# Lightning attention in front of an MLP: attention two chunks at a time on 64x64 PE tiles, 512-byte loads of k and v in one gated sequence, and dummy matmuls from the moment the identity exists

## The chip, the cores and the metric

One core of one Trainium2 chip. The metric is device time in microseconds of one execution (lower is better). All runs told here ended in the state "fast", but for one of the six with 256-byte runs, which is left out of its figures; the granted TensorE clock is 0.985 to 1.0 in the profiles, and the two places below 0.998 are named. A kernel's time is the median of its runs. Faster or slower needs more than 2%. The engines are PE (TensorE, matmuls), DVE (VectorE), ACT (ScalarE), POOL (GpSimd) and SP (SyncE, which issues transfers).

## The reference, cut to what matters

Causal linear attention with a decay per head, then a two-layer MLP over its output. Batch 4, 8 heads, 768 positions, head width 64; the MLP goes 512 → 2048 → 512 over 3072 tokens. All inputs and the output are float32.

```python
# attention, block by block of 64 positions (lam is one decay per head)
intra = einsum('bhic,bhjc->bhij', qb, kb) * Dmask        # lam^(i-j) for i >= j, else 0
intra = einsum('bhij,bhjd->bhid', intra, vb)
inter = einsum('bhid,bhde->bhie', qb * lam_pow, kv_state)
out   = intra + inter
kv_state = lam_block * kv_state + einsum('bhsd,bhse->bhde', kb * rev_pow, vb)
...
# MLP
h = x @ w_in
g = where(h >= 1, h, where(h <= -1, 0, (h + 1)**2 / 4))
out = g @ w_out
```

## The kernel before

Attention works on 24 chunks of 128 positions (six to a batch entry), the MLP on six stages of 512 tokens (four chunks). q is multiplied by lam^pos and k by lam^-pos while they are cast to bf16 (`cast_q`, `cast`), so that a plain causal mask suffices and the state is a plain sum. k and q are then transposed: by matmuls with an identity for the first six chunks, by DMA later. `xT` is the attention output, transposed, as the MLP reads it.

The kernel fixes the order itself: each operation is entered in a list with its engine, an estimated duration, what it needs and a due time, and a small list scheduler in Python fixes the order on each engine. Each engine's program then has its instructions in this order. What the change touches:

```python
ORDER = [0, 1, 2, 3, (0, 0), (0, 1), (0, 2), (0, 3), 4, (1, 0), ...]   # loads: chunks, (0,i) = w_in parts, (1,i) = w_out parts
PARTS = {1: 4, 2: 2, 3: 2, 4: 1}                 # MLP stage -> into how many token parts layer 1 is cut
L0 = [(0, 0), (0, 1), (1, 0), (1, 1), (0, 2), (1, 2), (0, 3), (1, 3)]   # stage 0: (half of the tokens, quarter of w_in)
...
def f_s2(c):                                     # scores of one chunk: two row tiles of 64 x 128
    for hp in range(HP):
        for hi in range(2):
            nc.tensor.matmul(pst[c, hi][:, hp, :], lhsT=kT[c][HD[hi], hp, :], rhs=q_cols(c, hp, HD[hi]), ...)

def f_o(c):                                      # output of one chunk: 4 + 8 full-array matmuls, block-diagonal operands
    for hp in range(HP):
        if cb > 0:
            nc.tensor.matmul(po[:, hp], lhsT=ubd[(c - 1) % NUB][:, hp, :], rhs=q_cols(c, hp), ...)
        for hi in range(2):
            nc.tensor.matmul(po[:, hp], lhsT=vi[c % NV][:, hp, hi].rearrange("p a d -> p (a d)"), rhs=sc_sb[c][:, hi, hp, :], ...)

def f_u(c):                                      # state: 4 matmuls, summed in PSUM over the whole batch entry
    for hp in range(HP):
        nc.tensor.matmul(pu[0][:, hp, :], lhsT=pair(ks[c], hp), rhs=v_pair(vi[c % NV], hp), ...)

def f_x(c):                                      # ACT: the output of chunk c goes to its columns of the stage's xT
    if sx not in xT:
        xT[sx] = xp.tile([128, KO, MS], BF16, name="xT", tag="xT")
    nc.scalar.copy(out=xT[sx][:, :, off:off + C]..., in_=pot[c]...)

def f_l1(s, ni, n, tok):                         # MLP layer 1
    for j in range(n):
        for ko in range(KO):
            nc.tensor.matmul(ph[:, j * m:(j + 1) * m], lhsT=w_in_sb[:, ko, ...], rhs=xT[s][:, ko, tok], ...)

def f_load(c, x, wait):                          # k and v after the first pair: per chunk, 64 floats = 256 bytes a run
    d = nc.sync.dma_start(out=t, in_=(k, v)[x - 1][b, :, s0:s0 + C, :].rearrange("h p d -> p h d"))
```

Of the kernel before, what the change touches and what calls it, by code (L numbers as in the profile page):

```python
# [23 lines left out]
def kernel(  # L24
# [18 lines left out]
    C = 128  # L43
# [12 lines left out]
    LD = 6  # L56
# [3 lines left out]
    DX, DLEAD = 16, 6000  # L60
# [3 lines left out]
    XT, NQT, NQK, RING = 6, 4, 4, 3  # L64
    W_IN = (4, 4, 4, 4)
    W_OF = [i for i, n in enumerate(W_IN) for _ in range(n)]
    ORDER = [0, 1, 2, 3, (0, 0), (0, 1), (0, 2), (0, 3), 4, (1, 0), (1, 1), 5, (1, 2), (1, 3)]
    PF = (0,)
    D0 = (8350, 11900, 15450, 19000)
    FIRST = [(0, 2), (2, 4)]  # L70
    L0 = [(0, 0), (0, 1), (1, 0), (1, 1), (0, 2), (1, 2), (0, 3), (1, 3)]
    GATE = {(0, 0): ("lq", 1), 4: 1, 6: 5}
    LORD = {0: (0, 1, 2), 2: (0, 1, 2)}
# [10 lines left out]
    scp = ctx.enter_context(tc.tile_pool(name="scp", bufs=3))  # L84
    xp = ctx.enter_context(tc.tile_pool(name="xp", bufs=3))
    xsp = ctx.enter_context(tc.tile_pool(name="xsp", bufs=2))
# [7 lines left out]
    pp_u = ctx.enter_context(tc.tile_pool(name="pp_u", bufs=1, space=PS))  # L94
    pp_s = ctx.enter_context(tc.tile_pool(name="pp_s", bufs=1, space=PS))
    pp_o = ctx.enter_context(tc.tile_pool(name="pp_o", bufs=1, space=PS))

# [12 lines left out]
    pos_i = const.tile([128, 2, NCB], I32)  # L110
    nc.gpsimd.iota(pos_i[:, 0], pattern=[[C, NCB]], base=-S // 2, channel_multiplier=1)
    nc.gpsimd.iota(pos_i[:, 1], pattern=[[1, 2], [2 * C, NCB // 2]], base=-S // 2, channel_multiplier=2)
# [4 lines left out]
    for e in range(2):  # L117
# [4 lines left out]
    causal = const.tile([128, 128], F32)  # L122
    nc.gpsimd.memset(causal, 1.0)
    nc.gpsimd.affine_select(
        out=causal, in_=causal, compare_op=AX.is_ge, fill=0.0,
        base=0, pattern=[[1, 2], [2, 64]], channel_multiplier=-1)


    NKB, NUB, NV = 2, 3, 4
    kbd = [const.tile([128, HP, 2, 128], BF16, name=f"kbd{i}") for i in range(NKB)]  # L130
    ubd = [const.tile([128, HP, 128], BF16, name=f"ubd{i}") for i in range(NUB)]
    vi = [const.tile([128, HP, 2, 2, D], BF16, name=f"vi{i}") for i in range(NV)]
# [4 lines left out]
    for t in vi[:2]:  # L137
        nc.vector.memset(t, 0.0)
    rest = const.tile([1, 3, H], F32)
    nc.scalar.activation(out=rest[:, 0], in_=lam_r, func=AF.Ln)  # L140
    pos = const.tile([128, 2, NCB], F32)
# [7 lines left out]
    ln_lam = ln_ps[:, 0, :H]  # L149
    for i in range(3):  # L150
        nc.tensor.matmul(ln_lam, lhsT=ones, rhs=piece[:, i], start=(i == 0), stop=(i == 2))
    nc.scalar.copy(vi[2], vi[0])
    arg = const.tile([128, 2, NCB, H], F32)
    nc.vector.tensor_tensor(arg.rearrange("p a c h -> p (a c) h"), _bc(pos.rearrange("p a c -> p (a c)"), 2, H),
                            _bc(ln_lam, 1, 2 * NCB), op=AX.mult)
    for t in ubd[:2]:
        nc.vector.memset(t, 0.0)
    tab_q = const.tile([128, 2, NCB // 2, H], F32)
    nc.scalar.activation(out=tab_q.rearrange("p a c h -> p (a c) h"), in_=arg[:, 1], func=AF.Exp)
    tab_p = const.tile([128, 2, 2, H], F32)  # L160
    nc.scalar.activation(out=tab_p.rearrange("p e m h -> p e (m h)"),
                         in_=arg[:, 1].rearrange("p (e m) h -> p e (m h)", e=2)[:, :, :2 * H], func=AF.Exp, scale=-1.0)
    tab_k = const.tile([128, NCB, H], F32)
    nc.scalar.activation(out=tab_k, in_=arg[:, 0], func=AF.Exp, scale=-1.0)
    nc.scalar.copy(vi[3], vi[1])
    tab_qn = const.tile([128, NCB, H], F32)
    causal_n = const.tile([128, 128], F32)

    def late_setup():
        nc.scalar.activation(out=tab_qn, in_=arg[:, 0], func=AF.Exp)  # L170
        nc.gpsimd.memset(causal_n, 1.0)
        nc.gpsimd.affine_select(out=causal_n, in_=causal_n, compare_op=AX.is_ge, fill=0.0,
                                base=0, pattern=[[1, 128]], channel_multiplier=-1)

    def v_out(t):

        a = list(t[:, 0, 0, 0, :].ap)
        return bass.AP(t.tensor, t[:, 0, 0, 0, :].offset, [a[0], [4 * D, HP], [3 * D, 2], [1, D]])

    def v_pair(t, hp):  # L180

        x = t[:, hp, 0, 0, :]
        return bass.AP(t.tensor, x.offset, [list(x.ap)[0], [3 * D, 2], [1, D]])

    def v_rows(t, hp, rows):

        x = t[rows, hp, 0, 0, :]
        return bass.AP(t.tensor, x.offset, [list(x.ap)[0], [3 * D, 2], [1, D]])
# [33 lines left out]
    MMS, FETCH = {"s": 8, "o": 12}, 1300  # L222
    FIRST_BYTE = 2350
    LDD, QXD, KXD, STD = 20000, 7000, 7000, 3000
    ON_POOL, ON_DVE = (1,), ((0, 1),)
    W_AFTER = {1: ("cq", 1, 1)}

    def run_plan(free):
# [25 lines left out]
        while len(out_seq) < len(ops):  # L254
# [12 lines left out]
            if x.dma:  # L267
                dma_free = max(dma_free, t + (1300 if e == "SP" else 2100)) + x.dma
                x.end = dma_free + (400 if x.key[0] in ("ld", "lq") and x.key[1] < (CPS if x.key[0] == "ld" else CPS // 2) else 1000 if x.key[:2] == ("w", 0) else 1400)
                if x.key[0] in ("ld", "lq") and x.key[1] >= (FAR if x.key[0] == "ld" else FAR // 2):  # L270
                    x.end += SLACK if (x.key[1] if x.key[0] == "ld" else 2 * x.key[1]) >= 10 else NEAR
                if e == "SP":
                    xfer.append(dma_free)
            out_seq.append((t, len(out_seq), x))
            for u in users[x.key]:
                left[u.key] -= 1
                if left[u.key] == 0:
                    ready[u.eng].append((max(y.t if y.eng == u.eng and y.key != u.gate else y.end + (XSL if u.eng == "SP" and y.eng == "POOL" and u.dma in (640, 1280) else LAT) for y in u.needs), u))
        for t, _, x in sorted(out_seq, key=lambda p: p[:2]):
            if DBG:  # L280
                print(f"{t / 1e3:9.3f} {x.due / 1e3:9.3f} {x.eng:5s} {x.ns:6.0f} {x.key}")
            x.fn()

    def mm(*cols):
        return sum(c / 2.4 + 3 for c in cols)
# [3 lines left out]
    pu = [None]  # L289
# [5 lines left out]
    def cast(c, eng):  # L295
        ks[c] = qkp.tile([128, H, D], BF16, name="ks", tag="ks")
        tab = tab_p[:, c % 2, c // 2] if c // 2 in PF else tab_k[:, c % NCB, :]
        eng.tensor_tensor(ks[c], qkv_ld[c, 1], _bc(tab, 2, D), op=AX.mult)  # L298

    def cast_q(m, e, eng):  # L300
        if e == 0:
            qs[m] = qsp.tile([128, 2, H, D], BF16, name="qs", tag="qs")
        qs[m, e] = qs[m][:, e]
        if 2 * m >= DX:
            eng.tensor_tensor(qs[m, e], qkv_ld[m, 0][:, e], _bc(tab_qn[:, (2 * m + e) % NCB, :], 2, D), op=AX.mult)  # L305
            return
        eng.tensor_tensor(qs[m, e], qkv_ld[m, 0][:, :, e], _bc(tab_q[:, e, m % (NCB // 2), :], 2, D), op=AX.mult)  # L307
# [6 lines left out]
    def q_cols(c, hp, rows=slice(0, 128)):  # L314

        i = c % 2
        if c >= DX:
            return qT[c // 2][rows, i, hp, :]
# [3 lines left out]
    vn, x_sb = {}, {}  # L322

    def cast_v(c):
        if c == CPS:
            late_setup()
        if c >= DX:
# [38 lines left out]
    def last_of(a):  # L366

        return a | 1 if a // 2 in PF else a

# [435 lines left out]
```

## Time and profile before

| | before |
|---|---|
| median of 3 runs | 219.13 us (218.85 to 219.54) |
| span in the profile | 217.3 us |
| first MLP matmul starts | 18.9 us |
| last matmul ends | 214.1 us |
| PE busy | 204.9 us, 94% |

The main views are shown and read in the prediction. Two more are needed for the comparison. First, the work by stretches of the kernel before, from the first MLP matmul on. The columns of the work by stretches are the stretch, its length, then the busy time (and the number of instructions) of PE, PE weight loads, DVE, ACT and POOL, the granted clock, the DMA share and GB/s; those of the order of time are start, duration, instruction, count, and in brackets the idle time before it with what ended it.

```profile
18.90:36.60 17.70, 16.87 (x170) 14.15 (x171) 13.71 (x21) 13.62 (x26) 8.20 (x10) 1.00 1.22 216
36.60:214.20 177.60, 177.24 (x1505) 110.13 (x1504) 113.43 (x174) 100.40 (x176) 43.04 (x37) 1.00 0.77 153
```

From 36.6 us on PE is idle for only 0.36 us in 177.6. What it loses, it loses before.

### The profile page before, as it was taken

Reading aid. Unit: us, or ns where it says so; the run is one execution under the profiler, and the core shown is the slowest. Engines: PE = TensorE matmul, PEld = TensorE weight load, DVE = VectorE, ACT = ScalarE, POOL = GpSimd, SP = SyncE. Lnnn points to the kernel's source line nnn. Section 1 sums busy time; section 2 is a strip of 40 time slices with the busy share of each in tenths; the row PEclk is TensorE's granted clock in tenths of the full one; section 3 lists DMA queues with packets and bytes.
Section 4 is the critical chain, followed back from the end, with each engine's and each line's share of the span. In section 5 each row is a group of like instructions: output and inputs, shape, how many; then the busy total and the mean of one; then the engine's idle time right before and its main releaser. Section 6 shows DMA issues by size and latency. Waiting matters only on the chain.

```text
span 217.3 us, 4494 instructions
## 1 busy us (share of the span) xinstructions
PE 204.9 (94%) x1803; PEld 132.8 (61%) x1803; DVE 139.4 (64%) x221; ACT 124.5 (57%) x222; POOL 62.3 (29%) x69
## 2 busy tenths in 40 slices
PE   0589899999999999999999999999999999999994
PEld 0378787778558777777767776744545544444442
DVE  5685697869926796958858776632688655554301
ACT  7457678357637677577657657635864544555030
POOL 5590096037533464341409200343000000000000
DMA  6999999989998999999998346999784301110122
GB/s 166 277 214 207 252 172 217 214 178 214 179 227 153 250 154 238 158 241 220 196 249 199 67 83 137 218 191 221 231 138 169 88 12 48 48 48 7 45 97 97
DMA packets 95974, 35.42 MB, mean 163 GB/s; under 512 B 78418, under 2 KB 93010, under 8 KB 95954
## 3 DMA queue, kind: packets, MB, share of 16 engines
q1 hardware_dynamic: 91728, 30.94, 69.9%
q0 software_dynamic: 4224, 4.19, 12.0%
q8 instruction: 14, 0.23, 0.5%
q14 instruction: 6, 0.05, 0.1%
q10 hardware_dynamic: 2, 0.00, 0.0%
HBM read 27.26 MB, written 6.29 MB: 154 GB/s over the span
## 4 chain that ended last, share of the span: by engine, by line
PE 92%; DMA 2%; ACT 2%; DVE 1%; issue 1%; POOL 1%; DVEq 0%; POOLq 0%
PE ph L481 39%; PE py L529 36%; PE po L439 3%; PE ps L409 3%; PE pu L380 2%; DMA x0f<-in_q_dram 2%; PE po L436 1%; PE py L523 1%; PE pt L336 1%; PE po L431 1%; PE po L457 1%; PE py L343 1%; PE po L428 1%; POOL qs L307 1%; ACT r L490 1%
## 5 line engine op out<-in xcount | busy, mean ns | idle before, releaser
L481 PE MATMUL ph<-xT,w_in_sb 128*128 128x256 bf16 (+2 forms) x768 | 95.7, 273 | 0.9 <-ACT xT L469 0.7
L490 ACT ACTIVATE r<-ph,one 128x512 bf16<-128x512 f32 x96 | 65.9, 688 | 46.3 <-PE ph L481 28.9
L529 PE MATMUL py<-w_out_sb,gT 128*128 128x512 bf16 x368 | 89.9, 379 | 0.0
L481 PEld LDWEIGHTS <-w_in_sb 128*128 128x128 bf16 x768 | 63.2, 98 | 23.9 <-issue 1.3
L529 PEld LDWEIGHTS <-gT 128*128 128x128 bf16 x368 | 34.9, 98 | 34.5
L500 DVE TENSOR_SCALAR t<-r 128x1024 bf16<-128x1024 bf16 x48 | 24.2, 505 | 35.8 <-ACT r L490 35.7
L506 DVE TENSOR_TENSOR w<-r,t 128x1024 bf16<-128x1024 bf16 x48 | 38.6, 803 | 1.4
L511 DVE TENSOR_TENSOR gT<-w,t 128x1024 bf16<-128x1024 bf16 x48 | 37.4, 780 | 1.7
L298 POOL TENSOR_TENSOR ks<-x1f,tab_k 128x512 bf16<-128x512 f32 x20 | 25.0, 1256 | 26.1 <-DMA x1f<-in_k_dram 20.5
L534 ACT COPY osb<-py 128x512 f32<-128x512 f32 x23 | 13.5, 586 | 17.7 <-PE py L529 16.4
L307 POOL TENSOR_TENSOR qs<-x0f,tab_q 128x512 bf16<-128x512 f32 x15 | 17.1, 1156 | 21.1 <-DMA x0f<-in_q_dram 15.9
L384 ACT CAST ubd<-pu 64x256 bf16<-64x256 f32 x40 | 14.6, 366 | 8.1 <-PE pu L380 5.2
L305 POOL TENSOR_TENSOR qs<-x0f,tab_qn 128x512 bf16<-128x512 f32 x8 | 9.0, 1126 | 28.6 <-DMA x0f<-in_q_dram 21.2
L421 DVE TENSOR_TENSOR sc<-ps,causal 128x512 bf16<-128x512 f32 x12 | 8.3, 689 | 9.5 <-PE pt L409 9.4
L469 ACT CAST xT<-po 128x512 bf16<-128x512 f32 x15 | 8.8, 584 | 8.8 <-PE po L439 5.2
L439 PE MATMUL po<-sc,vi 128*128 128x128 bf16 x112 | 10.5, 219 | 0.0
L439 PEld LDWEIGHTS <-vi 128*128 128x128 bf16 x112 | 8.4, 98 | 1.1
L421 DVE TENSOR_TENSOR sc<-ps,causal_n 128x512 bf16<-128x512 f32 x8 | 5.5, 691 | 5.0 <-PE pt L409 5.0
L436 PE MATMUL po<-qT,ubd 128*128 128x128 bf16 x48 | 8.7, 219 | 0.0
L331 ACT CAST vi<-x2f 128x512 bf16<-128x512 f32 x14 | 8.6, 614 | 0.0
L421 DVE TENSOR_TENSOR sc<-pt,causal 128x512 bf16<-128x512 f32 x12 | 8.2, 680 | 0.0
L409 PE MATMUL ps<-qT,kT 64*128 64x128 bf16 x80 | 7.9, 219 | 0.0
(89 smaller groups left out, 128.2 us busy)
## 6 DMA issues: line engine op xcount, KB each, us to landing
out_dram<-osb SPq DMA_DIRECT2D x23, 256.0 KB, 2.5
x1f<-in_k_dram SPq DMA_DIRECT2D x22, 256.0 KB, 5.1
x2f<-in_v_dram SPq DMA_DIRECT2D x22, 256.0 KB, 4.7
x0f<-in_q_dram SPq DMA_DIRECT2D x8, 512.0 KB, 5.5
w_in_sb<-in_moe_w_in_dram POOLq DMA_DIRECT2D x4, 512.0 KB, 7.9
w_out_sb<-in_moe_w_out_dram POOLq DMA_DIRECT2D x4, 512.0 KB, 7.7
x0f<-in_q_dram SPq DMA_DIRECT2D x8, 256.0 KB, 4.1
raw<-in_k_dram SPq DMA_DIRECT2D x1, 512.0 KB, 5.5
```

What stands on the lines that cost most here:

```text
L298: eng.tensor_tensor(ks[c], qkv_ld[c, 1], _bc(tab, 2, D), op=AX.mult)
L307: eng.tensor_tensor(qs[m, e], qkv_ld[m, 0][:, :, e], _bc(tab_q[:, e, m % (NCB // 2), :], 2, D), op=AX.mult)
L384: nc.scalar.copy(out=ubd[c % NUB][HD[hi], :, HD[hi]], in_=pu[0][HD[hi], :, HD[hi]])
L409: nc.tensor.matmul(pst[c, hi][:, hp, :], lhsT=kT[c][HD[hi], hp, :], rhs=q_cols(c, hp, HD[hi]), start=True, stop=True)
L421: nc.vector.tensor_tensor(sc_sb[c][:, g], pst[c, g], _bc(causal if c < DX else causal_n, 1, HP), op=AX.mult)
L439: nc.tensor.matmul(po[:, hp], lhsT=vi[c % NV][:, hp, hi].rearrange("p a d -> p (a d)"), rhs=sc_sb[c][:, hi, hp, :], start=(cb == 0 and hi ...
L481: nc.tensor.matmul(ph[:, j * m:(j + 1) * m], lhsT=w_in_sb[:, ko, (ni + j) * 128:(ni + j + 1) * 128], rhs=xT[s][:, ko, tok], start=(ko == 0 ...
L490: nc.scalar.activation(out=o, in_=x, func=AF.Relu, bias=one[:, 0:1])
L500: nc.vector.tensor_scalar(t, r, 0.5, 1.0, op0=AX.mult, op1=AX.min)
L506: nc.vector.tensor_tensor(w, r, t, op=AX.subtract)
L511: nc.vector.tensor_tensor(gT[s][:, f - RW * n:f, tok].rearrange("p (a b) m -> p a b m", a=RW), w.rearrange("p a (b m) -> p a b m", m=m), t ...
L529: nc.tensor.matmul(py_t[s, ms], lhsT=gT[s][:, ko, ms * 128:(ms + 1) * 128], rhs=w_out_sb[:, ko, :], start=(ko == 0), stop=(ko == FO - 1))
```

## The change

Its intent, in four parts:

1. **Attention by pairs of chunks on 64x64 tiles.** Pair m is chunks 2m and 2m + 1. The positions of a pair are interleaved by parity. 64 keys of one parity and a head width of 64 fill a quarter of the array, so that two heads by two chunks stand side by side. Per pair there are three blocks on PE: A (state times q, scores of one parity), B (the same for the other parity), C (scores times v), each with four quarter-array matmuls side by side. The state no longer stays in PSUM: DVE adds each update to a float32 tile in SBUF. For pairs 4 to 11 the state update rides in the block C ahead of it (`MERGED`).
2. **Loads.** k and v come per pair, so that a run is two rows, 512 bytes. One list holds all loads, and at each change between the two kinds (q, k, v from SP; weights from POOL) the next load is held until one two or three places back has landed.
3. **Dummy matmuls** of the identity with itself from the moment it is built, to have PE at full clock when the real work comes (39 of them).
4. **MLP cuts.** Stage 1 in two parts, not four; stage 3 in one, not two. Stage 0 takes three quarters of `w_in` for the first half of its tokens before it turns to the second half.

The core of the diff (helpers, the entries of the list scheduler and removed special cases for the last chunks are cut):

```diff
-    ORDER = [0, 1, 2, 3, (0, 0), (0, 1), (0, 2), (0, 3), 4, (1, 0), (1, 1), 5, (1, 2), (1, 3)]
+    MERGED = tuple(range(4,12))
+    ORDER = [0, 1, (0, 0), (0, 1), (0, 2), 2, (0, 3), (1, 0), (1, 1), (1, 2), (1, 3), 3]
-    L0 = [(0, 0), (0, 1), (1, 0), (1, 1), (0, 2), (1, 2), (0, 3), (1, 3)]
+    L0 = [(0, 0), (0, 1), (0, 2), (1, 0), (1, 1), (1, 2), (0, 3), (1, 3)]
+    BACK = {True: 3, False: 2}
-    PARTS = {1: 4, 2: 2, 3: 2, 4: 1}
+    PARTS = {1: 2, 2: 2, 4: 1}
...
+    px = pp_o.tile([128, 2, HP, 128], F32)
...
+    def warm(n, w):
+        for _ in range(n):
+            if hot[0] is None:
+                hot[0] = pp_h.tile([128, MS], F32, name="ph", tag="ph")
+            nc.tensor.matmul(hot[0][:, :w], lhsT=ident, rhs=_bc(ident, 1, w // 128), start=True, stop=True)
...
+    TILES = [(0, 0), (1, 1), (0, 1), (1, 0)]
+    def f_s(a, inter=None):                                  # scores: 16 quarter-array matmuls
+        for b in range(HP):
+            for r, i in TILES:
+                nc.tensor.matmul(pst[a, r][HD[i], b, :], lhsT=kT[a][HD[r], b, HD[i]], rhs=q_cols(2 * m + i, b, HD[r]), ...)
+            if b == 0 and inter is not None:
+                f_n(m, inter)
+    def f_n(m, phase):                                       # state times q: 8
+        for n in range(2):
+            for r, g in TILES: ...
+                    nc.tensor.matmul(px[HD[g], i, h // 2, :], lhsT=ub[(c - 1) % NUB][HD[r], h % 4, :], rhs=q_cols(c, h % 4, HD[r]), ...)
+    def f_c(m):                                              # scores times v: 32
+        for e in (1, 0):
+            for j in range(HP):
+                for i, g in TILES: ...
+                    nc.tensor.matmul(px[HD[g], i, j, :], lhsT=v_sb[(2 * m + e) % NV][HD[i], 2 * j + g, :], rhs=sc_sb[2 * m + e][HD[i], r, b, :], ...)
+    def f_sum(c):                                            # DVE
+            nc.vector.tensor_tensor(state, state, pu[c % 2], op=AX.add)
...
     def f_load(c, x, wait):
+            t = ld.tile([128, H, 2, D], F32, name=f"x{x}f", tag=f"x{x}f")
             i = (k, v)[x - 1][b, :, s0:s0 + 2 * C, :].rearrange("h (j e) d -> j h (e d)", e=2)
             d = nc.sync.dma_start(out=t.rearrange("p h e d -> p h (e d)"), in_=i)
-            t = ld.tile([128, H, D], F32, name=f"x{x}f", tag=f"x{x}f")
-            d = nc.sync.dma_start(out=t, in_=(k, v)[x - 1][b, :, s0:s0 + C, :].rearrange("h p d -> p h d"))
...
+        if n and sw != (xfers[n - 1][0] == "w"):
+            back = BACK[sw]
+            gate = GATE.get(x, xfers[n - back] if n >= back else None)
```

## The prediction

> **What bounds the kernel now.** I read the page first (busy shares, slices, chain), then the waits of the matmul engine, then the work by stretches, then the order of time around the first matmuls and around one score block, then the loads one by one.
>
> ```profile
> span 217.3 us, 4494 instructions
> PE 204.9 (94%) x1803; PEld 132.8 (61%) x1803; DVE 139.4 (64%) x221; ACT 124.5 (57%) x222; POOL 62.3 (29%) x69
> ...
> PE   0589899999999999999999999999999999999994
> ...
> DMA  6999999989998999999998346999784301110122
> ...
> PE 92%; DMA 2%; ACT 2%; DVE 1%; issue 1%; POOL 1%; DVEq 0%; POOLq 0%
> ```
>
> The chain that ends last is PE for 92% of the span, and DVE, ACT and POOL have slack. So an instruction taken off PE after the start is worth its own time, and one taken off another engine nothing. The DMA row is full for the first 22 slices (to about 120 us): early on, PE can run no further than the loads let it.
>
> ```profile
> PE py L343 <- POOL qs L307: 3.2, 1, 3.2
> PE ph L481 <- ACT xT L469: 0.7, 1, 0.7
> ```
> ```profile
> 0.00:6.80 6.80, 0.48 (x3) 0.30 (x3) 3.64 (x13) 3.96 (x8) 4.28 (x16) 1.00 0.75 191
> 6.80:18.90 12.10, 10.34 (x129) 8.23 (x130) 8.41 (x15) 6.50 (x14) 6.78 (x7) 1.00 1.28 232
> ...
> 42.00:100.00 58.00, 57.87 (x639) 42.14 (x637) 42.29 (x59) 36.29 (x65) 25.47 (x22) 1.00 1.14 201
> 100.00:200.00 100.00, 100.00 (x741) 57.18 (x740) 63.61 (x102) 58.78 (x103) 16.44 (x14) 1.00 0.61 134
> ```
>
> The first MLP matmul (L481) starts at 18.9 us; from 42 us on PE never waits. The last matmul ends at 214.1 us and 3.2 us of copy and store follow. So the kernel is three parts: 18.9 us of start, 195.2 us of dense PE, 3.2 us of tail.
>
> The dense part, from start-to-start spacings in the order of time: a matmul of 512 columns takes 0.216 us (8 in 1.73), of 256 columns 0.109 (16 in 1.75), of 128 columns 0.056 (32 in 1.79). MLP layer 1 is 128 x 0.216 + 384 x 0.109 + 256 x 0.056 = 83.9 us, layer 2 368 x 0.216 + 3.5 = 83.0, together 166.9. The attention in it, with one score block in view:
>
> ```profile
> 59.65 1.03 PE L529 MATMUL py<-w_out_sb,gT 128*128 128x512 bf16 x4
> 60.61 0.23 PE L409 MATMUL ps<-qT,kT 64*128 64x128 bf16 x1
> 60.61 0.23 PE L409 MATMUL pt<-qT,kT 64*128 64x128 bf16 x1
> ...
> 60.79 0.22 PE L409 MATMUL pt<-qT,kT 64*128 64x128 bf16 x1
> 60.94 0.60 PE L529 MATMUL py<-w_out_sb,gT 128*128 128x512 bf16 x2
> ```
>
> Two half-height matmuls start together and the four pairs are 0.056 apart, so the block should cost 0.22 us. But the full-array matmuls ahead should have been through at 60.52 (the group start plus 4 x 0.216) and the next starts at 60.94: 0.42. Entering and leaving the divided array costs about 0.10 us each. Rows after 18.9 us: L409 80 pairs x 0.056 + 20 blocks x 0.20 = 8.5; L439 112 x 0.056 = 6.3; L380 68 x 0.056 = 3.8; L436 48 x 0.056 = 2.7; L431 64 x 0.028 = 1.8; L428 28 x 0.056 = 1.6; transposes and L391 24 x 0.056 = 1.3. Sum 26.0. 195.2 - 166.9 - 26.0 = 2.3 us is idle time and small hitches, most of it before 42 us.
>
> The start. Until about 17.6 us PE runs at half rate:
>
> ```profile
> 9.62 0.31 PE L401 MATMUL ps<-qT,kT 64*64 64x128 bf16 x1 [0.52 <-DVE kT L353]
> 9.62 0.31 PE L401 MATMUL ph<-qT,kT 64*64 64x128 bf16 x1
> 9.63 0.31 PE L401 MATMUL ps<-qT,kT 64*64 64x128 bf16 x1
> 9.63 0.31 PE L401 MATMUL ph<-qT,kT 64*64 64x128 bf16 x1
> 9.73 0.31 PE L401 MATMUL ps<-qT,kT 64*64 64x128 bf16 x1
> ```
>
> Four quarter-array matmuls start together (9.62 to 9.63) and the next four 0.107 us later: four in the time of one, at twice the later 0.056. Loads, issue time plus time to landing: q 5.1, k 6.8, v 8.6 and the next q 10.5 us, all 512-byte runs, 1.83 us per 512 KB; then k, v, k, v in 256-byte runs at 11.7, 12.9, 14.2, 15.3, 1.2 us per 256 KB; then the weights at 10.83 + 6.6 = 17.4, 13.78 + 7.0 = 20.8, about 23.4 and 15.31 + 11.2 = 26.5.
>
> ```profile
> 10.83 0.93 POOL L199 DMA_DIRECT2D w_in_sb<-in_moe_w_in_dram  x1 [2.29 <-DMA x0f<-in_q_dram]
> ```
> ```profile
> w_in_sb<-in_moe_w_in_dram POOLq DMA_DIRECT2D x1, 512.0 KB, 6.6
> ```
>
> **What the Trainium skill says.** "TensorEngine Tiling (Array Packing)", Key Properties: changing the tiling mode drains the engine, and different tiles load and compute in parallel. The trace agrees: 0.10 us per change, four tiles at once. The same page, Restrictions and Gotchas: column tiling excludes fast weight load. No run here shows quarter-array matmuls at full rate, so whether four keep 0.056 us is open. "TensorE: Matmul & The Clock Gate", Part 1: the engine starts at half clock and is released after about 3.4 us of sustained activity; the trace agrees on the halves (0.107 against 0.056) but the release comes 9 us after the first real matmuls. "DMA: Bandwidth & Descriptors", Specifications: 512 bytes or more for line rate; the trace agrees, 286 GB/s (512 KB in 1.83 us) against 218 (256 KB in 1.2 us).
>
> **The change part by part.**
>
> (1) PE work. Per pair of chunks after the change: block A (8 inter, 16 score matmuls) is 6 groups of four x 0.056 + 0.20 = 0.54; B the same; C (32 output matmuls) 8 x 0.056 + 0.20 = 0.65; the state update 8 groups of 64 columns x 0.028 = 0.22, inside C's tile mode from pair 4 on, else 0.42. That is 1.95. Before, chunks 4 to 15: scores 0.84, output 24 x 0.056 = 1.34, state 0.45, together 2.63; chunks 16 to 23 already used the short form, output 0.90, together 2.19. So full tiling saves 0.7 on some pairs and little on the last four, because three mode changes of 0.20 replace two. The built order has, behind the first MLP matmul: B and C of pair 1 (1.2), 16 transposes (0.9), A, B, C of ten pairs (17.3), two lone updates (0.85) and eight merged ones (1.8): 22.0 against 26.0, minus 4.0. A of pair 1 has moved ahead of it, where PE idles.
>
> (2) MLP: stage 1 goes from four parts to two, stage 3 from two to one: 384 x 0.109 + 192 x 0.216 = 83.4, minus 0.5.
>
> (3) Start. The dummies warm PE from about 1.7 us (the identity is built by then). Pair 0, by measured durations: k at 6.8, both casts on DVE to 8.2, the k copy to 8.7, scores, masks. Then DVE meets the cast of the next k, in order ahead of the last mask, and waits for it (10.5 + 1.83 = 12.4); that mask ends near 13.7. C of pair 0 also stands behind a q transpose whose POOL cast, after the first weight issue, ends near 13.7. Then ACT has v, v, state, x, k copy, state, x in order behind v (14.2): seven steps of about 0.5 end at 17.9. The first weights land near 17.2. So the MLP starts at 18.0, 0.9 earlier. Halving the cold attention gains little: what it frees is spent waiting for loads.
>
> (4) Loads. k and v of one pair take 3.7 instead of 4.8 us. But the 3 MB ahead of the weights stay, and the second and third weights come near 20.8 and 23.4 as before. Pair 2 now goes before the fourth, so that one lands near 31; ten MLP blocks, the rest of pair 1 and the transposes fill PE to about 31. Idle time there I leave at 2.3 us as before: less from late copies, more from waits for weights.
>
> Sum: 18.0 + 166.4 + 22.0 + 2.3 = 208.7; tail 3.2 gives a span of 211.9; the 1.8 us between span and time (219.13 - 217.3) gives 213.7. I say 213.5.
>
> **The rivals.**
> (a) Weight loads without the fast path limit the small tiles. For it: the skill's restriction, and 64-column moving blocks leave only 0.028 us per four loads. Against it: in the cold block above loads hide at four per 0.107. If only the state update is held to 0.056 per group, ten updates x 0.22 add 2 us: 215.7. If all groups took 0.107, 10 x 28 groups x 0.05 add some 14 us: 227, slower.
> (b) A new wait takes the saving: A, masks, B, masks, C need a DVE turn of about 1.5 us (two masks 0.61 apart, each 0.69, plus latency) twice a pair, in the same two PSUM banks, and the built order leaves 1.7 to 2.6 us of MLP work between. An unlucky 2 us DVE operation ahead costs up to 0.5. Ten pairs at 0.2 make 2 us: 215.5.
> (c) The start gains more, because the dummies and the single load sequence let PE run without a hole to 42 us: idle falls to about 1, and 212 results.
> (d) The loads hide the start wholly (first weights near 18.5, holes at each weight): 214.5 to 215.
>
> **Range and chances.** The 2% line is 214.7. The arithmetic lies 1.2 below it, (a) in part, (b) and (d) put it just above, (c) below. The two-sided room is about 3: 210.5 to 217. Faster by over 2%: 0.68; within 2%: 0.28; slower: 0.04, for full (a).
>
> **What would show it.** Right: the first L441 matmul near 18 us and waiting for ACT or a weight landing; groups of four tiles 0.056 apart at full rate; about 0.20 us lost per tiled block; no PE waits over 0.5 us after 45 us; span near 212 with the same tail. Wrong: groups 0.1 apart, the state update over 0.4 us, PE waiting for masks in every pair, or the MLP starting before 17 or after 19 us.

## More of the kernel before

The order of time of PE: start, duration, instruction, count, and in brackets the idle time before it with what ended it.

```profile
23.67 1.04 PE L481 MATMUL ph<-xT,w_in_sb 128*128 128x256 bf16 x8
25.38 7.43 PE L481 MATMUL ph<-xT,w_in_sb 128*128 128x256 bf16 x64 [0.67 <-ACT xT L469]
```

MLP layer 1 waits 0.67 us for ACT to copy attention output into `xT`.

## The result, and the profile after

| | before | after |
|---|---|---|
| median, same rounds | 219.05 us (218.85 to 219.63, 6 runs) | 217.44 us (216.94 to 218.09, 6 runs) |
| ratio to before, 95% interval | 1 | 0.9923 (0.9901 to 0.9945) |
| span in the profile | 217.3 us | 215.8 us |
| first MLP matmul | 18.90 us | 19.18 us |

A ratio is the mean time of one kernel's fast runs over that of the other's in the same rounds, so it isn't quite the ratio of the medians. The change gains 0.8%: within 2%, and 217.44 lies above the predicted range of 210.5 to 217.

The page of the kernel after: span; busy times; the slices of PE and DMA; the chain that ended last.

```profile
span 215.8 us, 5410 instructions
...
PE 202.4 (94%) x2285; PEld 117.6 (54%) x2314; DVE 150.3 (70%) x235; ACT 116.5 (54%) x201; POOL 55.6 (26%) x60
...
PE   6887897999999999999999999999999999999993
...
PE 88%; DVE 6%; issue 2%; ACT 2%; POOL 0%; POOLq 0%; DVEq 0%
```

PE's share of the chain has fallen from 92% to 88%, and DVE's has risen from 1% to 6%. PE is the bound still, but something else has come into the chain. One warning: the trace has 2285 matmul records of 2314 issued (one weight load each). The 29 missing ones make gaps of about 0.2 us that the view calls "issue"; they aren't idle time, and the counts below are short for the same reason.

The waits of PE in the kernel after (total, times, longest):

```profile
PE px L374 <- ACT xT L430: 1.9, 2, 1.5
PE py L489 <- issue: 1.7, 11, 0.2
PE ph L151 <- POOL ident masks.py:199: 1.6, 1, 1.6
PE ph L441 <- ACT xT L430: 1.1, 1, 1.1
PE pt L324 <- ACT qT L334: 0.7, 1, 0.7
PE pt L331 <- ACT qT L334: 0.7, 1, 0.7
```

The wait for the identity is the first thing PE does, and the one of 1.5 us ends just before the MLP begins. The 11 of "issue" are the missing records. That leaves one wait of 1.1 us and two of 0.7 us, and the stretches of the same kernel say where they are:

```profile
19.18:36.00 16.82, 14.42 (x183) 11.73 (x176) 12.93 (x21) 11.21 (x18) 4.78 (x6) 1.00 1.17 219
36.00:212.60 176.60, 173.46 (x1876) 97.45 (x1904) 125.53 (x190) 94.82 (x161) 43.79 (x36) 1.00 0.69 149
```

Before, PE was idle for 0.83 us of its first 17.7 us after the MLP had begun (17.70 less 16.87); after, for 2.40 us of 16.82. They stand in the order of time of PE:

```profile
23.92 1.16 PE L441 MATMUL ph<-xT,w_in_sb 128*128 128x256 bf16 x9
26.12 6.39 PE L441 MATMUL ph<-xT,w_in_sb 128*128 128x256 bf16 x55 [1.05 <-ACT xT L430]
32.35 0.39 PE L331 MATMUL pt<-ident,qs 128*128 128x128 bf16 x4
33.41 0.38 PE L331 MATMUL pt<-ident,qs 128*128 128x128 bf16 x4 [0.67 <-ACT qT L334]
34.47 0.61 PE L324 MATMUL pt<-ident,ks 128*128 128x128 bf16 x8 [0.67 <-ACT qT L334]
```

And the copy that PE awaits at 26.12, in the order of time of ACT:

```profile
25.00 1.07 ACT L430 CAST xT<-px 128x512 bf16<-128x512 f32 x2 [0.86 <-PE ph L441]
```

Read the two together. Block C of pair 1 was through at 24.0 us, so ACT could have copied its two outputs then. ACT sat idle for 0.86 us instead and began at 25.00, released by an MLP matmul; then PE sat idle until the copies were done. Each waits for the other in turn. Later, PE transposes half of q of pair 2, waits for ACT to copy that half out, transposes the other half into the same PSUM tile, and waits again.

**A ledger of PE.** Busy times can't be added up here, as the ends of matmuls are modelled and records are missing. So I worked out, for each kernel, how long the issued sequence of matmuls takes at the start-to-start spacings that the traces show at full clock: 0.216 us for 512 columns, 0.109 for 256, 0.056 for 128, for a group of four tiles 0.056 (0.0315 with 64 columns), and 0.10 for each change of array mode. I call that the work. What the stretch from the first MLP matmul to the start of the last matmul has beyond it, I call holes. The reckoning is good to about 0.3 us: done again with just these spacings, the kernel before comes to 192.8 and 2.2, and the others agree within 0.1.

| us | before | after | difference |
|---|---|---|---|
| first MLP matmul | 18.90 | 19.18 | +0.3 |
| work | 192.5 | 187.5 | -5.0 |
| holes | 2.5 | 5.6 | +3.1 |
| last matmul starts | 213.88 | 212.37 | -1.5 |

So by this ledger the gain on PE is 5.0 us, and 3.1 us of it went into holes, of which 1.6 lie in blocks that start before 35.5 us (3.31 against 1.69) and 1.5 are spread over the dense part in pieces of under 0.4 us.

The 1.5 us in the dense part are mostly not idle time. The kernel with both splits and the ReLU first (below) has all its 2314 matmul records, and in its dense part PE never waits 0.15 us or more; yet the ledger counts 1.8 us of holes there (3.25 less 1.49). Block by block, each tiled block takes 0.03 us more than the ledger gives it (its first group takes 0.08, not 0.056), and the nine in which groups are half full, at the first and last pair of each batch entry, 0.08 or 0.15 more: 1.5 us together, and about 0.2 in the 20 blocks of the kernel before. This is work that the ledger leaves out. With it the change takes about 4 us off PE and not 5 (189.0 against 193.0), and the true holes grow by about 2 (from 2.0 to 4.1): 1.6 early, and a wait of 0.34 us for ACT at 103.9.

One of ten blocks in the dense part, in the order of time of PE of the kernel after (rows between are left out; those of L362 and L374 there are the groups of four):

```profile
61.59 1.24 PE L489 MATMUL py<-w_out_sb,gT 128*128 128x512 bf16 x5
62.76 0.24 PE L362 MATMUL ps<-qT,kT 64*64 64x128 bf16 x1
62.76 0.24 PE L362 MATMUL pt<-qT,kT 64*64 64x128 bf16 x1
...
63.01 0.28 PE L362 MATMUL ps<-qT,kT 64*64 64x128 bf16 x4
63.22 1.04 PE L489 MATMUL py<-w_out_sb,gT 128*128 128x512 bf16 x4
```

Five matmuls of 512 columns from 61.59 take until 62.67, and the tiled ones start at 62.76: 0.09 us for the change of mode. The 20 matmuls between 62.76 and 63.22 run in six steps, four of four and two of two, as the first chunk of a batch entry has no state: 6 x 0.056 = 0.34, and 0.12 for the change back and a longer first step (62.76 to 62.84). Four small tiles do run at 0.056 us a group.

The start, from the order of time of DVE and of POOL in the kernel after:

```profile
12.60 1.56 DVE L294 TENSOR_TENSOR ks<-x1f,tab_p 128x512 bf16<-128x512 f32 x1
14.09 0.68 DVE L423 TENSOR_TENSOR sc<-py,causal 128x512 bf16<-128x512 f32 x1
15.02 0.68 DVE L294 TENSOR_TENSOR ks<-x1f,tab_p 128x512 bf16<-128x512 f32 x1
```
```profile
12.55 1.06 POOL L302 TENSOR_TENSOR qs<-x0f,tab_q 128x512 bf16<-128x512 f32 x1
```

The cast of k at 12.60 takes 1.56 us, and the same cast at 15.02 takes 0.68. The first lies beside POOL's cast of q at 12.55, which starts 0.05 us earlier and lasts 1.06. "SBUF — State Buffer" of the Trainium skill, Who interferes with whom, says that a DVE instruction with two SBUF inputs contends with a GpSimd instruction that reads SBUF, and that the later one blocks. The trace agrees: 1.56 us is about the 1.06 of POOL and a bit less than the 0.68 of the cast alone, one after the other. The mask behind it ends at 14.77 and not at 13.7.

### The profile page after: what moved, and what is told of

It reads as the page before. It is cut to its first block, busy times and chain, and to the rows that moved or that the text cites. A ratio compares the mean times of both kernels' runs of the same rounds, so it can differ in the third digit from the quotient of the medians.

```text
span 215.8 us, 5410 instructions
## 1 busy us (share of the span) xinstructions
PE 202.4 (94%) x2285; PEld 117.6 (54%) x2314; DVE 150.3 (70%) x235; ACT 116.5 (54%) x201; POOL 55.6 (26%) x60
## 4 chain that ended last, share of the span: by engine, by line
PE 88%; DVE 6%; issue 2%; ACT 2%; POOL 0%; POOLq 0%; DVEq 0%
PE ph L441 37%; PE py L489 35%; PE ph L151 3%; PE px L390 3%; PE ps L362 2%; PE px L374 2%; DVE sc L423 2%; PE py L483 1%; PE ps L403 1%; DVE w L466 1%; DVE ks L294 1%; ACT xT L430 1%; ACT qT L334 1%; PE pt L324 1%; DVE gT L471 1%
## 5 line engine op out<-in xcount | busy, mean ns | idle before, releaser
L441 PE MATMUL ph<-xT,w_in_sb 128*128 128x256 bf16 (+1 forms) x570 | 94.5, 308 | 1.3 <-ACT xT L430 1.1
L441 PEld LDWEIGHTS <-w_in_sb 128*128 128x128 bf16 x576 | 54.9, 98 | 31.2 <-issue 1.2
L294 POOL TENSOR_TENSOR ks<-x1f,tab_p 128x512 bf16<-128x512 f32 x18 | 22.8, 1284 | 25.7 <-PE pt L403 21.1
L430 ACT CAST xT<-px 128x512 bf16<-128x512 f32 x24 | 13.1, 586 | 9.5 <-PE px L390 8.6
L317 ACT CAST v<-x2f 128x512 bf16<-128x512 f32 x24 | 13.7, 619 | 0.2
L151 PE MATMUL ph<-ident 128*128 128x512 bf16 (+1 forms) x39 | 9.5, 381 | 1.6 <-POOL ident masks.py:199 1.6
L362 PE MATMUL ps<-qT,kT 64*64 64x128 bf16 x184 | 10.8, 220 | 0.0
L418 ACT CAST ub<-state 128x256 bf16<-128x256 f32 x19 | 7.7, 406 | 5.0 <-DVE state L411 3.5
L362 PEld LDWEIGHTS <-kT 64*64 64x64 bf16 x384 | 7.8, 106 | 4.0 <-issue 3.8
L362 PE MATMUL pt<-qT,kT 64*64 64x128 bf16 x176 | 9.8, 219 | 0.0
L374 PE MATMUL px<-qT,ub 64*64 64x128 bf16 x152 | 6.4, 222 | 2.0 <-ACT xT L430 1.9
```

Of the source, the lines that this page charges most:

```text
L151: nc.tensor.matmul(hot[0][:, :w], lhsT=ident, rhs=_bc(ident, 1, w // 128), start=True, stop=True)
L294: eng.tensor_tensor(ho(ks[c])[:, bs], hs(qkv_ld[c, 1])[:, bs], ho(_bc(tab, 2, D))[:, bs], op=AX.mult)
L362: nc.tensor.matmul(pst[a, r][HD[i], b, :], lhsT=kT[a][HD[r], b, HD[i]], rhs=q_cols(2 * m + i, b, HD[r]), start=True, stop=True)
L430: nc.scalar.copy(out=o, in_=px[:, c % 2].rearrange("p h (e j) -> p h j e", e=2))
```

## The experiments

The theory after the first look: the PE work fell as reckoned, and the holes between 24 and 35 us took most of the missing gain. Its rivals: that the tiled blocks cost more than the ledger says; that the late first MLP matmul (19.18 us) sets the end; that one of the parts meant for the start (dummies, long runs, gates) costs more than it brings. All results were correct. Kernels were timed together with the kernel before on the same chip; its medians there were 219.0, 219.3, 219.2 and 219.2 us.

### Two tiles for the attention output of stage 0

```diff
-        if sx not in xT:
-            xT[sx] = xp.tile([128, KO, MS], BF16, name="xT", tag="xT")
+        if sx == 0:
+            if (0, c // 2) not in xT:
+                xT[0, c // 2] = big.tile([128, KO, 2 * C], BF16, name=f"xT0{c // 2}")
...
-                                 rhs=xT[s][:, ko, tok], ...
+                                 rhs=xT[s][:, ko, tok] if s else xT[0, tok.start // (2 * C)][:, ko, :], ...
```

> The changed kernel with one edit: the transposed attention output of the first 512 tokens lies in two tiles (one for each half) instead of one. Theory A (part of the saved PE time is given back at the copies of pair 1, because writing the second half waits for MLP matmuls that read the first half, and later ones of those wait for the copies): the 1.2 us hole of PE near 24.8 us goes, and the time falls by 0.8 to 1.2 us against the changed kernel, a ratio to the kernel before of about 0.988. Rival B (the holes only fill the time until the next weights land): the hole moves to the next weight and the ratio stays at 0.992.

Measured: 216.15 us (215.82 to 216.81, 5 runs), ratio 0.9868 (0.9847 to 0.9888), that is 0.0055 below the changed kernel's 0.9923. Holes 4.24 instead of 5.61 us. The order of time of PE at the same place:

```profile
23.34 0.64 PE L390 MATMUL px<-sc,v 64*64 64x128 bf16 x32
23.91 7.45 PE L446 MATMUL ph<-xT,w_in_sb 128*128 128x256 bf16 x64
```

The 64 matmuls run through without a break, and ACT's two copies start at 24.03 instead of 25.00. The two halves of `xT` share no element, but they shared a tile, and the waits are set by tile: the copies waited for matmuls that read the other half, and matmuls on the first half waited for copies into the second. The hole of 1.05 us is explained, and on the path that sets the end: taken away, the time falls by 1.3 us and the holes by 1.4.

### A PSUM tile for each half of q of pair 2

```diff
     def f_tq(m, e):
+        if m == 2:
+            if e == 0:
+                ptt["q", m] = {}
+            ptt["q", m][e] = pp_y.tile([128, 2, HP, 128], BF16, name="py", tag="py")
+            for hp in range(HP):
+                nc.tensor.transpose(out=ptt["q", m][e][:, e, hp, :], in_=pair(qs[m, e], hp), identity=ident)
+            return
```

> The changed kernel with one edit: the two q transposes of pair 2 go to two PSUM tiles of another pool instead of the two halves of the tile that the k transposes use next. Theory A (near 32 to 35 us PE waits twice 0.7 us for the copy out of the same PSUM tile before it may write the other half): these waits go and the time falls by 1.2 to 1.6 us, ratio about 0.986. Rival B (weights bound this stretch): the fourth weight block landed at 31.2 us and the first of layer 2 at 34.7 us, so PE would wait there instead and the time falls by less than 0.4 us.

Measured: 217.22 us (216.51 to 217.53, 6 runs), ratio 0.991 (0.9891 to 0.993). The two waits of 0.67 us are gone, but the holes fall only from 5.61 to 5.49. The order of time of PE shows what came in their place:

```profile
32.92 0.61 PE L324 MATMUL pt<-ident,ks 128*128 128x128 bf16 x8
34.46 1.03 PE L448 MATMUL ph<-xT,w_in_sb 128*128 128x256 bf16 x8 [0.93 <-ACT r L457]
```

The next MLP block needs a PSUM buffer that ACT's ReLU (`r`) must empty first. ACT does that only after the two copies of q, which stand ahead of it in its fixed order. The two PSUM waits (1.34 us) were therefore covers over a wait of two thirds their length, and the early holes fall by 0.42 only. Of these, 0.30 come back later: the wait for ACT at 103.9 us grows from 0.34 to 0.78 (at 103.7). That the transposes waited at all would fit "PSUM — Partial Sum Buffer" of the Trainium skill, PSUM bank collisions raise a hardware error, whose rule is to guard PSUM by bank and quadrant and not by address: the halves are different addresses of one tile, and with two tiles the waits vanish. No run here separates this from waits set by tile, as `xT` showed them in SBUF. And removing a wait isn't removing its time.

### Both together

The edit is the sum of the two above.

> Both edits, the two output tiles and the two PSUM tiles. Theory A: the gains add, 2.0 to 2.7 us less than the changed kernel, time near 215.0, ratio about 0.981. Rival B: together they run into the landings of the layer 2 weights (34.7, 37.2, 39.8, 42.3 us), so the sum is no more than about 1.2 us, ratio 0.987.

Measured: 215.56 us (215.5 to 215.67, 4 runs), ratio 0.984 (0.982 to 0.9859). Holes 3.75 us, 1.9 less than in the changed kernel, and the median is 1.9 us lower. The wait for the ReLU is still there, 0.82 us.

### The state update in blocks of its own

```diff
-    MERGED = tuple(range(4,12))
+    MERGED = ()
```

This is meant to give eight pairs of mode changes back.

> The changed kernel with the state updates of pairs 4 to 11 as blocks of their own instead of behind the output block: eight more entries into and exits from the divided PE array, no other work. Theory A (after about 36 us every us of PE counts, and a mode change pair costs 0.2 us): the time rises by 1.3 to 2.0 us against the changed kernel, ratio about 1.000. Rival C (the dense part has slack, and the saving of attention was never on the path): less than 0.4 us, ratio 0.992 to 0.994.

Measured: 218.95 us (218.15 to 219.23, 6 runs), ratio 0.9993 (0.9975 to 1.0012): 1.5 us slower than the changed kernel by the medians. But the edit did less than it was meant to. In five of the eight pairs the scheduler put the update right behind block C all the same, in one tiled block (at 65.81 us, for example); only three updates stand alone, at 78.52, 121.38 and 160.70. Three pairs of changes at 0.2 us make 0.6, and the profiled runs differ by just that (span 216.4 against 215.8). This agrees with the ledger, in which time on PE in the dense part is on the path one for one, but it is a single run. What makes up the other 0.9 us of the medians is not shown. In the profiled run the third weight landed at 24.16 us instead of 23.20, and PE waited for it, which it doesn't in the changed kernel:

```profile
24.21 1.16 PE L441 MATMUL ph<-xT,w_in_sb 128*128 128x256 bf16 x9 [0.30 <-DMA w_in_sb<-in_moe_w_in_dram]
```

The rival that the mode changes cost much more falls by the traces: some 60 of them in ten pairs, each 0.09 to 0.12 us.

### The start: one mask and one copy moved ahead

Two moves in the emitted order of DVE and ACT: the last mask of pair 0 goes ahead of the cast of k that runs beside POOL, and the copy of the second output right behind the first.

```diff
+        for key, at, after in [(('m', 1, 1), ('cast', 2, 1), 0), (('x', 1), ('x', 0), 1)]:
+            y = next(p for p in seq if p[2].key == key)
+            seq.remove(y)
+            seq.insert(next(i for i, p in enumerate(seq) if p[2].key == at) + after, y)
```

> The changed kernel with two swaps of instruction order: DVE does the last score mask of pair 0 before the cast of the next k (which waits for a load), and ACT copies both halves of pair 0's output one after the other instead of with the k copy and a state copy between them. Theory A (the start is set by these in-order waits, as step 3 of the prediction had it but shorter): the first MLP matmul comes 0.4 to 0.8 us earlier than 19.18 and the time falls by 0.3 to 0.7 us, ratio 0.989 to 0.991. Rival B (weights 2 and 3, landing at 20.7 and 23.2, take it back at once): the first matmul comes earlier but the time stays, ratio 0.992.

Measured: 217.33 us (216.66 to 218.3, 6 runs), ratio 0.9913 (0.9893 to 0.9933). The first MLP matmul moves from 19.18 to 18.41 us as wanted, and nothing comes of it: the holes grow from 5.61 to 6.12. In the order of time of PE:

```profile
24.11 1.16 PE L446 MATMUL ph<-xT,w_in_sb 128*128 128x256 bf16 x9 [0.89 <-DMA w_in_sb<-in_moe_w_in_dram]
26.31 6.39 PE L446 MATMUL ph<-xT,w_in_sb 128*128 128x256 bf16 x55 [1.05 <-ACT xT L435]
```

PE now reaches the third part of `w_in` before it has landed (24.06 us in this run), and so stands where it stood. In the changed kernel's profile that part lands at 23.20, just when PE arrives here (23.22); in the other profiles of its family that keep the gates and 512-byte runs it lands between 23.01 and 24.16. So the wait of 0.89 us belongs to this run, and whether the other five had it isn't on record. But the median of all six is only 0.1 us below the changed kernel's, which is within the noise, for a start 0.8 us earlier. The rival that the late start alone sets the end falls.

### Both tiles, and the ReLU ahead of the copies of q

To the two splits are added four moves in the emitted order: on DVE the two steps of the activation's product for the group whose buffer the ReLU needs go ahead of a cast of k, and on ACT two ReLUs go ahead of the first copy of q of pair 2.

```diff
+        for key, at, after in [(('g', 2, 1), ('cast', 4, 1), 0), (('g', 2), ('cast', 4, 1), 0),
+                               (('r', 10), ('qT', 2, 0), 0), (('r', 11), ('qT', 2, 0), 0)]:
```

> The two-tile kernel of both edits (ratio 0.984), with four moves more: on DVE the activation product of the third group goes ahead of the casts of pair 2's k, and on ACT the last two activations of the second half go ahead of the q copies of pair 2. Theory A (in that kernel PE still waits 0.8 us for an activation, because ACT and DVE stand behind casts that wait for loads): that wait goes and the time falls by 0.5 to 0.9 us against both edits, ratio about 0.981. Rival B (the weights then bind): PE waits for the fourth weight block (landing near 32) and the time falls by less than 0.3 us, ratio 0.983 to 0.985.

Measured: 214.94 us (214.53 to 215.25, 4 runs), ratio 0.9801 (0.9786 to 0.9817). Holes 3.25 us, of which 1.49 early: less than the kernel before has there (1.69). The waits of PE that are left, beside those ahead of the MLP:

```profile
PE py L337 <- DVE qs L307: 0.6, 1, 0.6
```

The wait for the ReLU is gone. This is the fastest kernel: 2.0% faster than before and 1.1% faster than the change (its interval crosses the 2% line, so it's unclear). The three steps took off 1.3, 0.6 and about 0.6 us of time by the medians, and the holes fell by 1.4, 0.5 and 0.5. (The last step compares two chips, on which the kernel before took 219.0 and 219.3.) So the holes of the early part cost what the ledger says.

### All of it

The kernel above with the two moves of the start as well.

> All edits together: both tiles split, the swaps at the start, and the four moves on DVE and ACT. Theory A: the whole of the unexpected loss of the early part (1.2 us later start, some 3 us of holes) is in these waits, so the time comes to about 214, ratio 0.977 to 0.979, near the predicted 213.5. Rival B: the weights bind after two of the edits and the time stays at 215 or above, ratio 0.982 to 0.984.

Measured: 215.01 us (214.53 to 216.43, 6 runs), ratio 0.9815 (0.9789 to 0.984): no better than without. Holes 3.24. The order of time of PE shows the next bound:

```profile
35.28 1.04 PE L506 MATMUL py<-w_out_sb,gT 128*128 128x512 bf16 x4 [0.37 <-DMA w_out_sb<-in_moe_w_out_dram]
```

PE now waits for the first part of `w_out`. With the late copies out of the way, the weights bind, and pushing the start further only waits for them.

### No dummy matmuls

```diff
     def warm(n, w):
-        for _ in range(n):
+        for _ in range(0):
```

> The changed kernel without its 39 dummy matmuls. Theory A (the dummies matter because the first real matmuls otherwise run at half clock until some us into the MLP): the tiled blocks before 19 us stand 0.107 us a group apart, so do the first MLP matmuls at twice their time, and the total rises by 1.5 to 3 us, ratio 1.000 to 1.006. Rival D (the start is bound by loads and copies, so the clock is of no matter, and the dummies even delay the first transposes): within 0.5 us, ratio 0.990 to 0.994.

Measured: 219.9 us (218.85 to 220.96, 6 runs), ratio 1.0028 (1.0003 to 1.0054), so the dummies are worth about 2.5 us by the medians. The first MLP block in the order of time of PE:

```profile
19.41 3.59 PE L441 MATMUL ph<-xT,w_in_sb 128*128 128x256 bf16 x16
```

The changed kernel runs the same 16 matmuls in 1.92 us. Without dummies PE enters the MLP at half rate.

### Dummy matmuls in the kernel before

The same helper and the same filling of PE's idle time, copied into the kernel before.

```diff
+    def warm(n, w):
+        for _ in range(n):
+            if hot[0] is None:
+                hot[0] = pp_h.tile([128, 512], F32, name="ph", tag="ph")
+            nc.tensor.matmul(hot[0][:, :w], lhsT=ident, rhs=_bc(ident, 1, w // 128), start=True, stop=True)
...
+        warm((8, 7, 2)[i], 128)
```

> The kernel before with only the dummy matmuls of the change added. Theory A (its start is bound by loads and by copies on other engines, the clock counts little): PE reaches full rate by about 8 us, the first MLP matmul comes at 18.2 to 18.7 instead of 18.9, the time falls by 0.2 to 0.8 us, ratio 0.996 to 0.999. Rival E (PE at half clock bounds its start, where it is busy for 10.3 of 12.1 us): the first MLP matmul comes at about 17.5 and the time falls by 1.2 us or more, ratio below 0.9945.

Measured: 218.94 us (218.66 to 219.16, 6 runs), ratio 0.9991 (0.9976 to 1.0005): nothing. In the order of time of PE:

```profile
18.88 1.05 PE L502 MATMUL ph<-xT,w_in_sb 128*128 128x256 bf16 x8 [1.18 <-DMA w_in_sb<-in_moe_w_in_dram]
```

PE was through with its attention at 17.70 us, 1.2 earlier than before, and waited 1.18 us for the first weights. These landed at 18.84 us here and at 17.44 in the kernel before, though both issue them at 10.8. A load of instructions (16 KB, queue q8) begins at 16.77 us here, with the weights on their way, and at 17.36 there; that it holds them up is likely, but was not tested. So the dummies do bring PE forward, and in this run the weights take it back. Without them, the work ahead of the MLP brings the kernel before to full rate by 18.1 us (matmuls of 128 columns 0.056 apart from 18.06), before its MLP starts. In the changed kernel it does not. That this comes from fewer and sparser matmuls ahead of the MLP is likely, but was not tested by itself. So the dummies prevent a loss in the changed kernel, and brought no gain to the one before.

### Runs of 256 bytes again

k and v of a pair as two transfers, one for each chunk, as before the change; the gates stay.

```diff
+            i = (k, v)[x - 1][b, :, s0:s0 + 2 * C, :].rearrange("h (j e) d -> e j h d", e=2)
-            d = nc.sync.dma_start(out=t.rearrange("p h e d -> p h (e d)"), in_=i)
             for e in range(2):
+                d = nc.sync.dma_start(out=t[:, :, e], in_=i[e])
```

> The changed kernel with k and v of each pair loaded by two transfers of 256-byte runs instead of one of 512-byte runs, everything else the same. Theory A (early, every transfer is on the path of the weights behind it): v of pair 1 lands 1.1 us later, the weights too, pair 2 costs 1.1 us again, and the time rises by 1 to 2.5 us, ratio 0.997 to 1.004. Rival (loads hidden behind PE): less than 0.4 us, ratio 0.990 to 0.994.

Measured: 223.40 us (222.31 to 224.73, 5 fast runs; the sixth, 226.21, is slow), ratio 1.0197 (1.0168 to 1.0226), 6.0 us slower than the changed kernel. v of pair 1 lands at 17.89 us instead of 14.07, the first weights at 20.17 instead of 17.60, and the MLP starts at 21.11 instead of 19.18. The waits of PE show a new one as well:

```profile
PE px L374 <- DMA qT<-qs: 1.6, 1, 1.6
```

Not all 6 us are the length of the runs: the split also makes twice as many transfers, and PE, having waited longer, was at half rate again (the first 16 MLP matmuls take 2.93 us; granted clock 0.992). But it shows that the long runs are needed to keep the start at 19 us in this order of loads.

### No gates

```diff
-            gate = GATE.get(x, xfers[n - back] if n >= back else None)
+            gate = None
```

> The changed kernel without the gates that hold a transfer back until an earlier one has landed (buffers and engine order alone still limit them). Theory A (the landings of the first weights set how far PE gets in the first 36 us): the loads of pair 2 go ahead of the weights, the first weights land at 22 us or later instead of 17.6, the first MLP matmul comes after 22 and the time rises by 2 to 4 us, ratio 1.002 to 1.010. Rival (order of the transfers does not matter, as the sum of bytes is the same and PE catches up): within 0.6 us, ratio 0.989 to 0.995.

Measured: 223.46 us (223.05 to 224.66, 6 runs), ratio 1.0207 (1.0181 to 1.0233), 6.0 us slower than the changed kernel. In the order of time of PE:

```profile
21.64 3.10 PE L441 MATMUL ph<-xT,w_in_sb 128*128 128x256 bf16 x16 [2.45 <-DMA w_in_sb<-in_moe_w_in_dram]
```

The first weights land at 21.60 us instead of 17.60, the second and third at 25.31 and 28.93 instead of 20.64 and 23.20: the loads of pair 2 are issued from 8.48 us on, and not from 20.66, and share the DMA engines with them. PE waits 2.45 us and falls to half rate (the 16 matmuls of that row take 3.10 us, against 1.92; granted clock 0.985). The gates, too, prevent a loss.

### The ledger over all runs

| kernel | first MLP matmul | work | holes | of them early | time |
|---|---|---|---|---|---|
| before | 18.90 | 192.5 | 2.50 | 1.69 | 219.05 |
| after | 19.18 | 187.5 | 5.61 | 3.31 | 217.44 |
| two output tiles | 19.17 | 187.5 | 4.24 | 2.60 | 216.15 |
| two q tiles | 19.16 | 187.5 | 5.49 | 2.89 | 217.22 |
| both | 19.13 | 187.5 | 3.75 | 2.00 | 215.56 |
| both, ReLU first | 19.22 | 187.5 | 3.25 | 1.49 | 214.94 |
| all | 19.00 | 187.5 | 3.24 | 1.67 | 215.01 |
| start moved | 18.41 | 187.5 | 6.12 | 4.27 | 217.33 |
| no dummies | 19.41 | 187.5 | 7.17 | 5.43 | 219.9 |
| 256-byte runs | 21.11 | 187.5 | 9.55 | 4.88 | 223.40 |
| no gates | 21.64 | 187.5 | 8.99 | 6.24 | 223.46 |
| before, with dummies | 18.88 | 192.5 | 2.67 | - | 218.94 |

All in us. "Early" are holes in blocks that start before 35.5 us; half-rate matmuls count as holes. The kernel without merged state updates would have about 188.1 of work, for its three blocks more, and 5.7 of holes.

## Why the prediction was right or wrong

**What bounds the kernel: right.** PE bounds it before and after, and time on PE in the dense part counts about one for one: the early holes taken off by the splits shorten the time by as much, and three tiled blocks more lengthen the profiled span by 0.6 us.

**Steps (1) and (2), PE work: right.** Predicted -4.0 and -0.5, so -4.5; measured -5.0 by the ledger, about -4 with the time of the tiled blocks that it leaves out. Groups of four tiles run 0.056 us apart at full rate, a mode change costs 0.09 to 0.12 us. Rival (a), weight loads that hold the small tiles back, is false: the lone updates with 64 columns run at 0.031 us a group. Rival (b), PE waiting for masks in every pair, is false as well: after 36 us the longest wait is 0.34 us, at 103.9, and it's for ACT and not for a mask. The smaller pieces, 1.5 us more than before by the ledger, are mostly the time of the tiled blocks themselves.

**Step (3), the start: wrong by 1.2 us, and moving it gained nothing.** Predicted 18.0, measured 19.18. The weights landed as predicted (17.60, 20.64, 23.20 and 31.20 against "near 17.2", 20.8, 23.4 and "near 31"). The term that failed is the last mask: the cast of k ahead of it was taken at 0.69 us and took 1.56 beside POOL, so that the mask ended 1.1 us later. The path from there isn't the predicted one, though: ACT's seven steps, reckoned from the landing of v at 14.2, took as long as predicted but began at 14.99, behind a copy of q, and ended at 18.67; and what came late through DVE was the second cast of k (15.02) with the state update behind it. The experiment moves mask and copy together, so it doesn't weigh them apart. But with the start at 18.41 it gains nothing. Adding the start to the rest of the sum was therefore an error of its own: an earlier start need not carry through, and in that run the third weight took it back. (One reading in the prediction is off as well: full rate came at 18.06 us, 11.3 after the first transposes at 6.81, not 9 us after the first real matmuls.)

**Step (4), "Idle time there I leave at 2.3 us as before: less from late copies, more from waits for weights": this is the step that failed.** The holes measure 5.6 us, 3.3 more (4.1 and 1.8 more without the time of the tiled blocks that the ledger leaves out), and the direction within the sentence is the wrong way round: in the changed kernel no wait for a weight shows after the MLP has begun, and the late copies have grown. The wait for `xT` was 0.67 us and is 1.05; the transposes of the two halves of q of pair 2, which in the kernel before had a block of MLP matmuls between them and a wait of 0.16 us, now follow each other directly, and they and the transposes of k behind them wait 2 x 0.67 us; and behind these lay the wait for the ReLU. The experiments take them off one at a time, and the time falls with them to 214.94, inside the predicted range.

Together: predicted end of PE 208.7 = 18.0 + 166.4 + 22.0 + 2.3. Measured, in the same terms: 19.18 + 187.53 + 5.61 and 0.2 for the last matmul itself, 212.5. That is +1.2 for the start, -0.9 for the work, +3.3 for the holes and 0.2 for the last matmul, 3.8 us in all; with the blocks' own time counted as work, +0.6 for the work and +1.8 for the holes. The tail (3.2) and the distance from span to time (1.75 in the profiled run, against 1.8) were right.

Rival (c) is the mirror of what happened: it expected the single load sequence and the dummies to take holes away. Rival (d), the loads hiding the start, gave 214.5 to 215. The experiment with all moves shows weights as the next bound: once the copies are out of the way, PE waits for `w_out`, at 215.0 us.

What stays open: the 0.9 us of the median without merged updates that three blocks don't explain, what moves the landing of the third weight between 23.0 and 24.2 us, what delays the first weights in the kernel before with dummies, and how much of the losses without gates and with 256-byte runs is the clock and how much the loads.

## What to carry to other kernels

When PE work is removed from a kernel that is dense on PE, don't carry the idle time over as a constant: look at each wait that is there already and ask whether the work that hid its remainder is among the work removed. A tile written in halves and read in halves ties the halves together: give each half its own tile, and then look for the wait that the first one covered, since here one of two splits alone gained next to nothing. A part of a change that is needed to hold the start (dummies, gates, long runs: 2.5 to 6 us lost without each) isn't a gain over a kernel that had no such loss.

## What the Trainium skill lacked or had wrong

- "TensorEngine Tiling (Array Packing)", Restrictions: column tiling excludes fast weight load; a figure is lacking. Little cost of it shows here: four 64x64 tiles with 128 moving columns each, every one with a weight load of its own, run a group in 0.056 us, as long as one full-array matmul takes, and with 64 columns in 0.031 us (0.029 in the full array); only the first group of a block takes 0.08.
- The same page, Key Properties, says that a change of mode drains the engine, without a figure. Here it is 0.09 to 0.12 us for each change.
- "TensorE: Matmul & The Clock Gate", Part 1: full rate after about 3.4 us of sustained activity. In the kernel before, with transposes and quarter-array matmuls and waits between them, full rate came at 18.06 us, 11.3 after the first transposes (6.81); with 39 dummies from 1.6 us on, transposes are 0.055 us apart at 7.55. The page names no share of busy time that counts as sustained, so this can't be reckoned from it.
- "SBUF — State Buffer", Who interferes with whom, has the rule for DVE and POOL right; a duration was missing: a cast of 128x512 takes 1.56 us instead of 0.68 when it starts 0.05 us after POOL's cast of 1.06 us.
